# A gated MLP behind linear attention on one core: the whole order of work is written anew

## The chip, the core and the metric

The kernel runs on one core of a Trainium2 chip. The core has a matrix engine (TensorE; PE in the profile, and PEld for its weight loads), VectorE (DVE), ScalarE (ACT), GpSimd (POOL) and SyncE (SP). Each engine takes its own instructions in order, and the engines meet only through semaphores. Here SP issues the loads of q, k and v, the DMA transposes and the stores; GpSimd issues the transfers of the weights. The metric is the device time of one execution in microseconds: lower is better. Three runs of the kernel before gave 149.77, 148.20 and 149.54 us, a median of 149.54.

## What is computed

q, k and v have the shape (4, 8, 768, 64): four batches, eight heads, 768 tokens, 64 columns. Each head has a decay `lam`. First comes linear attention with decay in blocks of 64 tokens, with a running state per head; its output, with the heads side by side, is a matrix of 768 x 512 per batch, and goes through a gated MLP with a spatial product:

```python
for b in range(nb):                      # blocks of 64 tokens
    intra = (qb @ kb.T * Dmask) @ vb
    inter = (qb * lam_pow) @ kv_state
    out[b] = intra + inter
    kv_state = lam_block * kv_state + (kb * rev_pow).T @ vb

h = relu(x @ w_in)                       # 512 -> 1024
u, v = h[:, :512], h[:, 512:]
v_n = (v - mean(v)) / sqrt(var(v) + 1e-6)
v_s = w_spatial @ v_n + b_spatial        # over the 768 tokens
out = (u * v_s) @ w_out                  # 512 -> 512
```

## The kernel before

The tokens are cut into 12 steps of 256 tokens, three to a batch: step n belongs to batch n // 3. A step has all eight heads. Matrix products run in bf16 with sums in fp32. PSUM has eight banks; bank 7 keeps the running state, and the other seven are handed from one piece of work to the next.

The program is a long string, `ORDER`, of 663 short tokens. A loop goes through it and calls for each token one small function, which gives one piece of work to one engine. The token names the function, then the step (or batch) and part, then the PSUM banks, and at the end the engine: T is TensorE, D VectorE, A ScalarE, P GpSimd, S SyncE. So `MK.0.1.0.1.D` is MK for step 0, half 1, from banks 0 and 1, on VectorE. The string alone sets the order on each engine and, for copies, which engine does them; the waits follow from what reads and writes what. The names, in the order in which a step goes through them:

- LQ, LK, LV load a step's q, k, v (512 KB each) into one of three buffers. WI.0 and WI.1 bring the half of W_in for v and that for u; WS.0 and WS.1 the halves of the spatial weights, WO the output weights, BS the bias. GT makes GpSimd wait until a load has landed.
- KM multiplies k by its decay, QC casts q, VC casts v. The work of KM and QC is cut in halves of heads (part 0 and 1; part 2 is both).
- For steps 0 to 4 TK and TQ transpose k and q on TensorE, EK copies the result from PSUM, and EQ copies it and multiplies it by the table that LT writes. For steps 5 to 11 QM multiplies q on VectorE or GpSimd, and DK and DQ transpose by DMA, issued by SP. The transposed k and q have two buffers each, so step n writes where step n - 2 was read.
- SC makes the scores (16 matmuls of 64 x 64), MK multiplies them by the mask. KV adds to the state, SS copies the state out of bank 7. AV.n.0 and AV.n.1 make the output of attention, and FN stands between them; EX copies it into xT.
- PV projects on the half of W_in for v (one 128-token tile each), PU on the half for u (all 256 tokens of two column groups). EV and EU apply relu out of PSUM. BN, RA, RD and VN normalise v.
- WT transposes the spatial weights and EW copies them. When the three steps of a batch are through VN, its eight PW (column group f, token half i) do the spatial product on top of the bias that GP put into the bank; each PW reads the six tiles of its batch that VN wrote. GM multiplies by u.
- PO makes an output tile of 128 tokens from four GM, EO copies it, ST stores it. PH, EH and SH are the same for half a tile, at the end.

The order interleaves three batches at once: while the PW of one batch run, attention for the next has begun, and the PO of the one before are fitted in between.

Of the kernel before, what the change touches and what calls it, by code (L numbers as in the profile page):

```python
# [26 lines left out]
TK.2.1.4.T EK.2.1.4.D EK.2.0.2.A SC.2.0.0.1.T MK.2.0.0.1.D SC.2.1.3.4.T MK.2.1.3.4.D EV.0.0.5.A RA.1.A BN.0.0.D
RA.0.A RD.1.D LV.5.S RD.0.D PU.1.0.6.T PU.1.1.2.T KV.2.0.T SS.2.0.A EU.1.0.6.A AV.2.0.0.1.T FN.2.0.1.D VN.0.0.D
VN.0.1.D PU.0.1.3.T EU.0.1.3.A KM.4.0.P AV.2.1.0.1.T EX.2.0.0.A EX.2.1.1.D GP.0.0.0.4.A EU.1.1.2.A GP.0.0.1.5.A
PU.0.0.6.T EU.0.0.6.D PV.2.0.3.T KM.4.1.P EV.2.0.3.A BN.2.0.D PV.2.1.0.T EV.2.1.0.A BN.2.1.D VN.1.1.D VN.1.0.D  # L30
WT.0.0.1.T WT.1.0.2.T EW.1.0.2.A RA.2.A EW.0.0.1.A RD.2.D VN.2.0.D WT.2.0.6.T EW.2.0.6.A PU.2.0.3.T GP.0.2.0.0.A
PU.2.1.2.T VN.2.1.D WT.1.1.1.T PW.0.0.0.4.T EU.2.0.3.A EU.2.1.2.A EW.1.1.1.A WT.2.1.6.T EW.2.1.6.A GP.0.3.0.3.D
GM.0.0.0.4.D GP.0.1.1.2.A PW.0.2.0.0.T GM.0.2.0.0.D GP.0.1.0.4.A WT.0.1.1.T EW.0.1.1.D PW.0.3.0.3.T TK.3.2.6.T
EK.3.2.6.A TQ.3.2.0.T PW.0.1.0.4.T GM.0.1.0.4.D EQ.3.2.0.D PW.0.1.1.2.T GM.0.1.1.2.D GM.0.3.0.3.D PW.0.0.1.5.T
GM.0.0.1.5.D KV.3.0.T SC.3.0.0.1.T MK.3.0.0.1.D SC.3.1.2.3.T MK.3.1.2.3.D GP.0.2.1.4.A PW.0.2.1.4.T TK.4.2.6.T
QC.4.2.A TQ.4.2.5.T EQ.4.2.5.D GM.0.2.1.4.D GP.0.3.1.0.A PW.0.3.1.0.T AV.3.0.1.2.T FN.3.1.2.D SS.3.0.A KV.3.1.T
KM.5.1.P EK.4.2.6.A SC.4.0.3.4.T GM.0.3.1.0.D KM.5.0.D DK.5.S AV.3.1.1.2.T EX.3.1.2.A EX.3.0.1.A SC.4.1.5.6.T
MK.4.1.5.6.D PO.0.2.0.T EO.0.2.0.A PO.0.4.2.T EO.0.4.2.D QM.5.1.P QM.5.0.D DQ.5.S VC.5.P PO.0.3.1.T PU.3.0.5.T
PV.3.1.6.T PV.3.0.0.T VC.4.A SS.3.1.D KV.4.0.T MK.4.0.3.4.D AV.4.0.2.3.T EV.3.0.0.D BN.3.0.D PO.0.5.4.T
EU.3.0.5.A SS.4.0.A KV.4.1.T EV.3.1.6.A BN.3.1.D LK.6.S KM.6.0.P FN.4.2.3.A AV.4.1.2.3.T EX.4.1.3.D SS.4.1.A  # L40
LV.6.S EX.4.0.2.A RA.3.A RD.3.D PO.0.1.0.T EO.0.1.0.A EO.0.3.1.A KV.5.0.T SC.5.0.5.6.T MK.5.0.5.6.D SC.5.1.2.3.T
# [40 lines left out]
"""


# [475 lines left out]
```

## Time and profile before

| | |
|---|---|
| median of three runs | 149.54 us (148.20 to 149.77) |
| the profiled execution, its own time | 150.31 us |
| its span, first to last instruction | 148.6 us |
| mean granted clock of TensorE | 0.977 |
| TensorE busy | 130.3 us (88% of the span) |
| VectorE, ScalarE, GpSimd busy | 112.8, 83.5, 46.9 us |
| read from and written to HBM | 24.77 and 6.29 MB |
| chain that ended last | TensorE 76%, VectorE 5%, issue 2%, ScalarE 2%, DMA 1% |

The span is what the profiler sees of one execution; the execution's own time has some 1.7 us more around it. Busy time of an engine is time in which at least one of its instructions runs. The chain is followed back from the last instruction, at each step to what released it; "issue" in it is time in which an engine waited for nothing that the profile shows. In the profile's rows an engine's name with a q behind it is its sequencer, which issues DMAs.

### The profile page before, as it was taken

To read this page: it belongs to the slowest core of one execution; us is meant where nothing else is said; L and a number is where in the kernel's file an instruction comes from. 1 tells how busy PE (TensorE), PEld (TensorE's weight loads), DVE (VectorE), ACT (ScalarE), POOL (GpSimd) and SP (SyncE) were. 2 spreads that over 40 slices of the span, in tenths; PEclk is the share of its full clock that TensorE was granted. 3 is DMA by queue.
4 is the path that set the end of the run, shared out by engine and by line. 5 is a ranking of instruction groups with operands and counts; after the bars stand their busy time and mean duration, and the time that the engine had idled before them with its cause. 6 is when DMAs were issued, how large, how long until landed. Compare 5 with 4: busy or idle time off the path is not lost.

```text
span 148.6 us, 4597 instructions
## 1 busy us (share of the span) xinstructions
PE 130.3 (88%) x1933; PEld 84.0 (57%) x1946; DVE 112.8 (76%) x214; ACT 83.5 (56%) x167; POOL 46.9 (32%) x59
## 2 busy tenths in 40 slices
PE   0287368999999999999999999799998999999990
PEld 0166343585776755566766656567663565666530
DVE  4467937798957998799989978967794898696720
ACT  3895710758985474695752658768404446742041
POOL 7593932029600090235050802670822000000000
PEclk9999965999999999999999999999999999999999
DMA  3999999999997015999997999989999487100524
GB/s 88 345 347 346 229 277 220 216 302 292 261 273 210 6 44 113 289 347 242 248 141 225 241 236 349 263 240 259 254 283 137 153 342 294 76 4 0 207 104 183
DMA packets 58376, 32.28 MB, mean 217 GB/s; under 512 B 15859, under 2 KB 55283, under 8 KB 58355
## 3 DMA queue, kind: packets, MB, share of 16 engines
q1 hardware_dynamic: 55968, 29.23, 75.4%
q0 software_dynamic: 2384, 2.75, 10.7%
q8 instruction: 15, 0.25, 0.6%
q14 instruction: 7, 0.05, 0.1%
q10 hardware_dynamic: 2, 0.00, 0.0%
HBM read 24.77 MB, written 6.29 MB: 209 GB/s over the span
## 4 chain that ended last, share of the span: by engine, by line
PE 76%; DVE 5%; issue 2%; ACT 2%; DMA 1%
PE ps L486 21%; PE ps L422 14%; PE ps L460 12%; PE ps L497 12%; PE ps L397 4%; PE ps L367 3%; PE ps L350 3%; PE ps L388 2%; PE ps L319 2%; DVE a_sb L355 2%; PE ps L472 1%; DMA out_dram<-o_sb 1%; DVE vn L451 1%; DVE st L437 1%; DVE xT L178 1%
## 5 line engine op out<-in xcount | busy, mean ns | idle before, releaser
L486 PE MATMUL ps<-wt_sb,vn 128*128 128x384 bf16 x192 | 33.5, 326 | 0.0
L289 POOL TENSOR_TENSOR kc<-k_in,lv 128x512 bf16<-128x512 f32 x18 | 19.3, 1082 | 39.8 <-PE ps L367 12.7
L355 DVE TENSOR_TENSOR a_sb<-ps,m 128x1024 bf16<-128x1024 f32 x24 | 28.7, 1215 | 2.3 <-PE ps L350 2.2
L422 PE MATMUL ps<-win_sb,xT 128*128 128x512 bf16 x92 | 24.6, 401 | 1.4 <-DVE xT L178 1.0
L486 PEld LDWEIGHTS <-vn 128*128 128x128 bf16 x192 | 18.3, 98 | 11.8 <-DVE vn L451 0.6
L460 PE MATMUL ps<-xT,win_sb 128*128 128x256 bf16 x192 | 23.5, 273 | 0.0
L497 PE MATMUL ps<-wout_sb,gT 128*128 128x512 bf16 x83 | 21.9, 380 | 1.2 <-issue 0.9
L492 DVE TENSOR_TENSOR gT<-ps,uT 128x384 bf16<-128x384 f32 x32 | 16.6, 550 | 5.8 <-PE ps L486 4.9
L460 PEld LDWEIGHTS <-win_sb 128*128 128x128 bf16 x192 | 18.1, 98 | 3.9
L437 DVE BATCH_NORM_STATS2 st<-vh 128x6 f32<-128x512 bf16 x24 | 16.5, 688 | 4.6 <-ACT vh L427 4.5
L176 ACT ACTIVATE ps<-bsp 128x384 f32<-128x384 f32 x26 | 12.5, 496 | 9.6 <-DVE gT L492 6.4
L176 ACT ACTIVATE o_sb<-ps 128x512 f32<-128x512 f32 x18 | 10.5, 596 | 12.0 <-PE ps L497 10.5
L427 ACT ACTIVATE vh<-ps 128x512 bf16<-128x512 f32 x19 | 11.3, 595 | 10.3 <-PE ps L422 10.0
L289 POOL TENSOR_TENSOR qc<-q_in,lqn 128x512 bf16<-128x512 f32 x11 | 11.9, 1087 | 15.7 <-DMA q_in<-in_q_dram 8.7
L422 PEld LDWEIGHTS <-xT 128*128 128x128 bf16 x96 | 9.6, 103 | 12.3 <-issue 2.5
L497 PEld LDWEIGHTS <-gT 128*128 128x128 bf16 x92 | 8.3, 98 | 9.9 <-issue 1.0
L176 ACT ACTIVATE xT<-ps 128x512 bf16<-128x512 f32 x15 | 8.5, 595 | 8.1 <-PE ps L397 8.1
L397 PE MATMUL ps<-a_sb,vb 64*64 64x128 bf16 x384 | 11.1, 222 | 1.6 <-issue 1.6
L176 ACT ACTIVATE s_sb<-ps 128x256 bf16<-128x256 f32 x17 | 6.5, 380 | 9.3 <-PE ps L367 9.3
L451 DVE TENSOR_SCALAR vn<-vh,mv,rstd 128x512 bf16<-128x512 bf16 x24 | 11.4, 506 | 0.2
L367 PE MATMUL ps<-vb,kc 64*64 64x64 bf16 x320 | 8.5, 193 | 3.1 <-DVE vb L178 1.8
L427 ACT ACTIVATE uT<-ps 128x512 bf16<-128x512 f32 x17 | 9.8, 590 | 1.7 <-PE ps L460 1.7
(70 smaller groups left out, 159.6 us busy)
## 6 DMA issues: line engine op xcount, KB each, us to landing
k_in<-in_k_dram SPq DMA_DIRECT2D x12, 512.0 KB, 5.7
q_in<-in_q_dram SPq DMA_DIRECT2D x12, 512.0 KB, 6.1
v_in<-in_v_dram SPq DMA_DIRECT2D x12, 512.0 KB, 6.7
out_dram<-o_sb SPq DMA_DIRECT2D x23, 256.0 KB, 3.8
wsp_raw<-in_moe_w_spatial_dram POOLq DMA_DIRECT2D x2, 576.0 KB, 12.4
win_sb<-in_moe_w_in_dram POOLq DMA_DIRECT2D x2, 512.0 KB, 9.5
wout_sb<-in_moe_w_out_dram POOLq DMA_DIRECT2D x1, 512.0 KB, 8.9
bsp<-in_moe_b_spatial_dram SPq DMA_DIRECT2D x1, 384.0 KB, 13.4
```

The costliest lines, as they stand in the source:

```text
L176: nc.scalar.activation(out=o, in_=i, func=AF.Copy)
L289: vec(e).tensor_tensor(out=dst[n % NCA][:, u].rearrange("p u m o d -> p o (u m) d"), in0=src[n % NIN].rearrange("p (o u) m d -> p o u m d" ...
L355: nc.vector.tensor_tensor(out=a_sb[n % NA][:, i].rearrange("p o w j x -> p o w (j x)"), in0=ps[:, b0:b1 + 1:b1 - b0].rearrange("p o (w y) ...
L367: nc.tensor.matmul(out=pkv[row(o), u], lhsT=kc[n % NCA][row(c), u, m, o, :], rhs=vb[n % NCA][row(c), 4 * o + u, m, :], start=new and u == ...
L397: nc.tensor.matmul(out=po[c ^ o][row(w), c, i], lhsT=vb[n % NCA][row(c), 4 * o + u, j, :], rhs=a[row(c), i, o, w, j, :], start=(r == 0 and ...
L422: nc.tensor.matmul(out=bank(b), lhsT=x[:, slot(c, g)], rhs=win_sb[:, g, DH:DFF], start=(g == 0), stop=(g == NCH - 1))
L427: nc.scalar.activation(out=o, in_=i, func=AF.Relu)
L437: nc.vector.bn_stats(out=st6[p2][:, t], in_=vh[p2][:, t])
L460: nc.tensor.matmul(out=pu[:, f2].rearrange("p (c x) -> p c x", c=2), lhsT=win_sb[:, g, f * P:(f + 1) * P], rhs=x[:, slot(0, g):slot(1, g) ...
L486: nc.tensor.matmul(out=bank(b)[:, 0:HW], lhsT=vn[bb % 2][:, s, f * P:(f + 1) * P], rhs=wt_sb[:, s, i * HW:(i + 1) * HW], start=False, stop ...
L492: nc.vector.tensor_tensor(out=gT[bb % 2][:, f, cols], in0=bank(b)[:, 0:HW], in1=uT[bb % 2][:, f, cols], op=ALU.mult)
L497: nc.tensor.matmul(out=bank(b), lhsT=gT[bb % 2][:, f, t * P:(t + 1) * P], rhs=wout_sb[:, f, :], start=(f == 0), stop=(f == NCH - 1))
```

## The change

Only the string `ORDER` differs. Both have the same 663 tokens up to their banks and engines, so the same loads, products, copies and stores. What moves:

- The loads begin with q of steps 0 and 1, then k of both, v of 0, k and q of 2, v of 1. Before it was k and q of 0, k and q of 1, v of 0 and 1.
- The transposes of steps 0 and 1 stand in one run of eight on TensorE, ahead of all scores. Before, scores and transposes of steps 0 and 1 took turns.
- GpSimd casts the four halves of q of steps 0 and 1 first, then one KM, and then issues WI.0, WI.1 and WS.0 one behind the other. Before, casts and multiplications stood between these.
- 86 tokens change engine. VectorE is given in net terms five SS, four VC, three GP, two EK, one KM, one QC, one EU and one EW, and gives away one EX, one EV and one EO. ScalarE has 13 operations fewer, GpSimd two.
- Banks are dealt out anew.
- From step 3 on the interleaving differs too: SC of steps 6 and 7 come earlier among the PW of batch 1, SC of step 11 stand closer behind AV of step 9, and at the end all PW of batch 3 come ahead of all its PH and PO. `one` (a table that nothing reads) moves from the first place to near the end.

The diff, cut to its head, to the parts that the prediction speaks of, and to the end:

```diff
--- before.py
+++ after.py
 ORDER = """
-one.D lam.A LK.0.S msk.P mkc.D LB.0.T LN.0.A posk.P LL.D LX.A KM.0.0.D pos.P idn.P TK.0.0.1.T KM.0.1.P
-TK.0.1.2.T LQ.0.S QC.0.1.D TQ.0.1.3.T LT.0.A QC.0.0.P TQ.0.0.4.T EQ.0.0.4.D LT.1.A EQ.0.1.3.D LK.1.S KM.1.1.P
-TK.1.1.5.T EK.0.0.1.A SC.0.0.3.4.T EK.0.1.2.A LQ.1.S QC.1.0.P EK.1.1.5.A GT.1.1.P WI.0.P KM.1.0.D LV.0.S
-SC.0.1.0.1.T LV.1.S TK.1.0.6.T EK.1.0.6.A TQ.1.0.2.T LQ.2.S LK.2.S QC.1.1.P TQ.1.1.5.T MK.0.0.3.4.D EQ.1.0.2.D
-MK.0.1.0.1.D VC.0.A KV.0.0.T AV.0.0.3.6.T SS.0.0.A FN.0.3.6.A LV.2.S QC.2.1.P BS.S LK.3.S GT.1.2.P WI.1.P
-EQ.1.1.5.D SC.1.1.0.1.T SC.1.0.4.5.T MK.1.0.4.5.D KV.0.1.T SS.0.1.A KM.2.0.P GT.2.1.P WS.0.P LQ.3.S LT.2.A
-AV.0.1.3.6.T LV.3.S LK.4.S VC.1.D KV.1.0.T LQ.4.S SS.1.0.A KV.1.1.T KM.2.1.P LK.5.S MK.1.1.0.1.D AV.1.0.2.4.T
-QC.2.0.A TQ.2.1.5.T EX.0.1.6.D WS.1.P TQ.2.0.0.T EQ.2.0.0.D LQ.5.S VC.2.P FN.1.2.4.A AV.1.1.2.4.T LV.4.S
-EX.1.0.2.D EQ.2.1.5.D EX.1.1.4.A PV.1.0.1.T EX.0.0.3.D SS.1.1.D PV.0.1.6.T EV.0.1.6.A PV.1.1.0.T EV.1.1.0.A
...
-PW.2.1.1.6.T GM.2.1.1.6.D AV.9.0.0.1.T SC.10.0.2.3.T SC.10.1.4.5.T KV.10.1.T FN.9.0.1.D AV.9.1.0.1.T DQ.11.S
-MK.10.0.2.3.D PO.2.2.6.T EO.2.2.6.D ST.1.1.S ST.2.2.S PO.2.5.2.T EX.9.1.1.A EX.9.0.0.A PV.9.0.3.T EV.9.0.3.D
-MK.10.1.4.5.D EO.2.5.2.A PO.1.3.6.T EO.1.3.6.D PV.9.1.1.T EV.9.1.1.A BN.9.1.D SS.10.1.A PO.2.0.0.T EO.2.0.0.A
-ST.2.0.S AV.10.0.3.4.T VC.11.P SC.11.1.5.6.T SC.11.0.1.2.T KV.11.0.T SS.11.0.D FN.10.3.4.A AV.10.1.3.4.T
...
+LQ.0.S msk.P idn.P lam.A LQ.1.S mkc.D pos.P posk.P LB.0.T LN.0.A LK.0.S LK.1.S LL.D LV.0.S QC.0.1.P LX.A
+QC.1.0.P QC.1.1.P QC.0.0.P KM.0.0.D LK.2.S TQ.1.0.1.T LT.1.A LT.0.A KM.1.1.P EQ.1.0.1.D TK.0.0.2.T TQ.0.1.3.T
+KM.0.1.D EK.0.0.2.D KM.1.0.D TK.0.1.4.T EK.0.1.4.A TQ.1.1.5.T TQ.0.0.6.T LT.2.A GT.1.1.P TK.1.0.0.T TK.1.1.1.T
+EQ.0.1.3.D VC.0.D EQ.1.1.5.D WI.0.P EQ.0.0.6.D KV.0.0.T SC.0.1.2.3.T LQ.2.S WI.1.P SC.0.0.4.5.T EK.1.1.1.D
+EK.1.0.0.A MK.0.0.4.5.D SC.1.1.0.1.T LV.1.S SS.0.0.A KV.0.1.T MK.0.1.2.3.D WS.0.P SS.0.1.A SC.1.0.4.5.T KM.2.0.P
+TK.2.0.6.T QC.2.0.A MK.1.1.0.1.D QC.2.1.D VC.1.A AV.0.0.2.3.T FN.0.2.3.A MK.1.0.4.5.D LV.2.S KV.1.0.T LK.3.S
+KM.2.1.P TQ.2.0.0.T AV.1.0.1.4.T FN.1.1.4.A AV.0.1.2.3.T SS.1.0.D AV.1.1.1.4.T EX.1.1.4.A GT.1.2.P WS.1.P
+TQ.2.1.5.T KV.1.1.T EX.1.0.1.D EX.0.1.3.D EX.0.0.2.D PV.1.1.4.T GT.2.1.P TK.2.1.1.T PV.0.0.3.T EV.1.1.4.A
+EK.2.1.1.D PU.1.0.2.T PV.1.0.4.T LV.3.S BS.S EK.2.0.6.A SS.1.1.D EQ.2.0.0.D VC.2.D BN.1.1.D EQ.2.1.5.D KV.2.0.T
...
+LQ.5.S KV.3.0.T VN.2.0.D LK.5.S PU.2.0.5.T VN.2.1.D PW.0.0.0.0.T EU.2.1.6.D GP.0.0.1.6.D EU.0.0.2.A GP.0.2.0.2.A
+PW.0.1.0.3.T QC.4.2.P QC.3.2.D EU.2.0.5.D TQ.3.2.4.T PW.0.0.1.6.T EK.3.2.1.A GM.0.0.0.0.D QM.5.1.P PW.0.2.0.2.T
...
+AV.5.0.0.1.T GP.1.0.0.3.D EV.4.0.6.A VC.6.D FN.5.0.1.D SS.5.0.A PO.0.0.4.T KV.6.0.T EV.4.1.2.A AV.5.1.0.1.T
+PU.4.1.5.T BN.4.0.D EX.5.1.1.A BN.4.1.D PU.4.0.6.T KM.7.1.D VC.7.D RD.3.D EX.5.0.0.A RA.4.A DQ.6.S DK.6.S
+PV.5.1.2.T PV.5.0.1.T RD.4.D VN.4.1.D PU.3.1.0.T EU.4.0.6.A EV.5.1.2.A VN.3.0.D PU.5.1.6.T EU.4.1.5.D VN.4.0.D
+QM.7.0.P EV.5.0.1.A BN.5.1.D EO.0.0.4.A BN.5.0.D SS.6.0.A EU.3.1.0.A DQ.7.S RA.5.A KM.7.0.P VN.3.1.D DK.7.S
+SC.6.0.1.2.T KV.6.1.T RD.5.D SC.6.1.4.5.T LV.8.S VN.5.0.D VN.5.1.D PU.5.0.0.T LK.8.S EU.5.1.6.A MK.6.1.4.5.D
+GP.1.2.1.6.A MK.6.0.1.2.D EU.5.0.0.A KM.8.1.P GP.1.1.1.0.A PW.1.2.1.6.T PW.1.0.0.3.T GP.1.3.1.4.A SS.6.1.D
...
+PW.2.3.0.3.T AV.9.0.0.4.T SC.10.0.5.6.T KV.10.1.T SC.10.1.1.2.T FN.9.0.4.D AV.9.1.0.4.T EX.9.0.0.A GM.2.3.0.3.D
+DQ.11.S VC.11.D EX.9.1.4.A PO.2.1.3.T PO.2.5.0.T SS.10.1.D MK.10.1.1.2.D EO.2.1.3.A PO.1.3.4.T PV.9.0.3.T
+SC.11.1.1.2.T MK.10.0.5.6.D SC.11.0.5.6.T EO.1.3.4.A KV.11.0.T MK.11.1.1.2.D MK.11.0.5.6.D EO.2.5.0.A EV.9.0.3.A
...
+GP.3.3.1.4.A GM.3.2.1.0.D ST.2.4.S PW.3.3.1.4.T PW.3.1.1.2.T PW.3.2.0.3.T GP.3.0.0.6.D GM.3.3.1.4.D ST.2.2.S
+GM.3.1.1.2.D PW.3.1.0.5.T PW.3.0.0.6.T PH.3.5.1.0.T GM.3.3.0.1.D GM.3.1.0.5.D one.D PO.3.4.4.T EO.3.4.4.A
+PO.3.3.2.T GM.3.0.0.6.D GM.3.2.0.3.D ST.3.4.S EH.3.5.1.0.D PH.3.5.0.1.T EH.3.5.0.1.D EO.3.3.2.A PO.3.1.5.T
+EO.3.1.5.D PO.3.0.6.T EO.3.0.6.D SH.3.5.1.S SH.3.5.0.S PO.3.2.3.T ST.3.3.S ST.3.1.S ST.3.0.S EO.3.2.3.A ST.3.2.S
...
```

More of the change, by code (lines that the diff above doesn't have):

```diff
@@ L27 @@
[L27 to L41, printed above, removed]
@@ new lines @@
+SC.4.0.2.3.T KM.5.1.P SS.4.0.A SC.4.1.4.5.T AV.3.1.1.6.T EX.3.0.1.D KV.4.1.T DQ.5.S MK.4.1.4.5.D EX.3.1.6.A
+PO.0.4.0.T PV.3.1.6.T PV.3.0.1.T PO.0.3.4.T EV.3.1.6.A PU.3.0.5.T MK.4.0.2.3.D AV.4.0.2.6.T EV.3.0.1.A
+EO.0.4.0.A VC.5.D BN.3.1.D KM.6.1.D FN.4.2.6.A DK.5.S BN.3.0.D SS.4.1.A EU.3.0.5.D LQ.7.S PO.0.5.3.T KM.6.0.P
+LV.6.S EO.0.3.4.A AV.4.1.2.6.T KV.5.0.T EX.4.1.6.D EO.0.5.3.A LK.7.S QM.6.0.P SC.5.0.0.1.T SC.5.1.4.5.T
+PO.0.1.3.T EX.4.0.2.A PV.4.1.2.T QM.7.1.P MK.5.0.0.1.D EO.0.1.3.A PV.4.0.6.T RA.3.A LV.7.S MK.5.1.4.5.D
@@ new lines @@
+VC.8.A PW.1.1.0.0.T PV.6.0.1.T PV.6.1.6.T GM.1.3.1.4.D EV.6.0.1.A LK.10.S EV.6.1.6.A AV.7.0.2.3.T LK.11.S
+SC.8.1.4.5.T GM.1.1.0.0.D SC.8.0.0.1.T FN.7.2.3.A MK.8.1.4.5.D KV.8.0.T AV.7.1.2.3.T EX.7.1.3.D MK.8.0.0.1.D
+PO.1.5.6.T ST.0.0.S ST.0.3.S EX.7.0.2.A PU.6.1.4.T PO.1.4.5.T LQ.11.S BN.6.0.D AV.8.0.2.3.T VC.9.P PO.1.0.0.T
+FN.8.2.3.D SS.8.0.D KV.9.0.T EO.1.4.5.D AV.8.1.2.3.T KM.10.1.P QM.9.1.D EU.6.1.4.A PV.7.1.1.T LQ.10.S EX.8.0.2.A
+BN.6.1.D KM.10.0.P LV.10.S GP.2.3.1.4.D PU.7.1.5.T PV.7.0.2.T EV.7.1.1.D BN.7.1.D EX.8.1.3.A QM.9.0.P PV.8.0.3.T
@@ new lines @@
+RA.6.A RD.6.D DK.9.S EV.7.0.2.A EO.1.0.0.A PU.8.1.1.T SS.9.0.A PV.8.1.2.T EV.8.0.3.A VN.6.0.D BN.7.0.D
+EV.8.1.2.A EO.1.5.6.A BN.8.0.D RA.7.A KV.9.1.T PU.6.0.0.T BN.8.1.D DQ.9.S VN.6.1.D GP.2.0.1.3.A QM.10.0.P
+EU.6.0.0.A RD.7.D VN.7.1.D VN.7.0.D RA.8.A LV.11.S PO.1.1.2.T RD.8.D PO.1.2.6.T VC.10.P SS.9.1.D VN.8.0.D
+VN.8.1.D QM.11.1.P PU.7.0.0.T QM.10.1.D EU.8.1.1.D EU.7.1.5.A PU.8.0.5.T EU.7.0.0.A EU.8.0.5.A GP.2.1.0.0.D
+ST.0.5.S GP.2.2.1.1.A EO.1.1.2.A PW.2.0.1.3.T PW.2.3.1.4.T DQ.10.S GM.2.0.1.3.D PW.2.2.1.1.T KV.10.0.T DK.10.S
```

62 lines of the change are left out of this document (25 added, 37 removed).

## The prediction

> **What bounds the kernel now.** I read the utilisation rows first, then busy time by stretch, then the chain of work in order of time. The page's rows:
>
> ```profile
> PE 130.3 (88%) x1933; PEld 84.0 (57%) x1946; DVE 112.8 (76%) x214; ACT 83.5 (56%) x167; POOL 46.9 (32%) x59
> ...
> q8 instruction: 15, 0.25, 0.6%
> ...
> qT<-qc SPq DMA_TRANSPOSE x7, 4.6
> ```
>
> Busy time by stretch (start:end, its length, then busy us and instructions of PE, PEld, DVE, ACT, POOL, granted clock, DMA share, GB/s):
>
> ```profile
> 0.00:23.00 23.00, 11.33 (x259) 8.77 (x260) 14.11 (x25) 13.62 (x29) 14.72 (x27) 0.93 1.03 270
> 23.00:30.00 7.00, 6.50 (x59) 3.22 (x59) 5.28 (x11) 3.21 (x5) 1.03 (x1) 0.75 1.15 218
> 30.00:140.00 110.00, 107.63 (x1596) 69.80 (x1606) 91.84 (x177) 64.24 (x130) 31.16 (x31) 1.00 0.85 209
> ```
>
> From 30 to 140 us TensorE is busy 107.6 of 110 us: it is the bound there, and all but 2.4 us is work that the change leaves as it is. Before 23 us it is busy 11.3 of 23, and from 23 to 30 its clock is at 0.75. So there are three places where a new order can gain or lose: the first 23 us, the 2.4 us of holes in the dense part, and new holes.
>
> The chain of work in order of time (start, length, what), its dense part:
>
> ```profile
> 94.15 0.81 issue
> ...
> 99.13 2.62 PE ps L460 x24
> 101.75 4.88 PE ps L486 x30
> ...
> 112.82 0.55 issue
> ...
> 116.14 0.86 PE ps L422 x4
> 117.00 0.86 PE ps L497 x4
> 117.86 0.24 PE ps L388 x8
> 118.10 0.22 PE ps L397 x16
> 118.32 0.45 PE ps L350 x32
> 118.77 0.18 PE ps L367 x12
> ```
>
> The rows run end to end: no operand is late. They also give the price of each piece of TensorE work at full clock: PV and PO 0.86, PU 2.62/3 = 0.87, PW 4.88 x 6/30 = 0.98, AV 0.24 + 0.22 = 0.46, SC 0.45/2 = 0.23, KV 0.18 x 16/12 = 0.24. The two large holes are "issue", where TensorE waits for nothing that another engine does.
>
> I read these two as instruction fetch. TensorE has 1946 weight loads and as many matmuls, and 15 packets carried instructions: 259 instructions, some 129 pairs, in a packet. Counted along the order, the hole at 94.15 stands behind about 1383 pairs (inside AV.8.1), that at 112.82 behind about 1634 (inside PO.2.2) and an early one, shown below at 19.77, behind about 223 (inside AV.1.0). Their distances are 1160 and 251 pairs, 9 and 2 packets: all three stand where a packet ends. By the prices above, the packet's worth of pairs ahead of them holds 5.0, 5.7 and 1.9 us of work, less than any other packet of this order (5.9 and up). Runs of 64x64 matmuls use up instructions fast, and the next packet comes too late.
>
> **The change, part by part.** No instruction is added or removed; all 663 steps stand in both orders. Work changes engine and place.
>
> *TensorE in the dense part.* Both orders have 17 runs of KV, SC and AV behind the first PW, and the same sums. What shifts is which work falls into which packet. In the new order the packets that hold pairs 1248 to 1376 and 1504 to 1632 carry 7.0 and 7.5 us instead of 5.0 and 5.7, and the shortest behind the head is 5.6 (pairs 608 to 736), then 6.2. A packet of 5.9 showed no hole before. I take both holes as gone: 0.81 + 0.55 = **-1.36 us**. The ends: nothing gained if the packet of 5.6 and those of 6.2 stop in their stead, all of it if none does; I take the end to which the row of 5.9 without a hole is nearer.
>
> The Trainium skill, "Runtime: NRT & Kernel Launch", section "Instruction fetch mechanics", says that the sequencer fetches the next block while it runs this one, so that crossing a block boundary is mostly hidden. By that rule the holes have another cause and stay, and the term is 0 instead of -1.36. The trace speaks for blocks of the size that the page gives, but against "hidden": three ends of packets have a hole.
>
> *The head.* Rows of the timeline (start, length, engine, line, what; in brackets the idle time before it):
>
> ```profile
> 1.94 1.37 SPq L191 DMA_DIRECT2D k_in<-in_k_dram  x1
> ...
> 10.16 0.92 POOL L247 DMA_DIRECT2D win_sb<-in_moe_w_in_dram  x1
> ...
> 16.14 1.15 DVE L178 CAST vb<-v_in 128x1024 bf16<-128x1024 f32 x1
> 16.68 0.63 POOL L243 COPY seen<-v_in 1x1 f32<-1x1 f32 x1
> ...
> 19.77 0.32 PE L397 MATMUL ps<-a_sb,vb 64*64 64x128 bf16 x3 [0.80 <-issue]
> ...
> 21.93 0.69 DVE L178 CAST xT<-ps 128x512 bf16<-128x512 f32 x1 [0.35 <-PE ps L397]
> ...
> 22.67 0.61 PE L422 MATMUL ps<-win_sb,xT 128*128 128x512 bf16 x1 [0.83 <-DVE xT L178]
> ```
>
> The issue groups, for the load at 1.94 and for the first half of W_in (last column: us from issue to landing):
>
> ```profile
> k_in<-in_k_dram SPq DMA_DIRECT2D x1, 512.0 KB, 5.8
> ```
>
> ```profile
> win_sb<-in_moe_w_in_dram POOLq DMA_DIRECT2D x1, 512.0 KB, 9.6
> ```
>
> And VectorE's groups from 6 to 23 us (count, busy us, mean ns, idle before):
>
> ```profile
> L355 DVE TENSOR_TENSOR a_sb<-ps,m 128x1024 bf16<-128x1024 f32 x4 | 4.9, 1219 | 0.9 <-PE ps L350 0.7
> L333 DVE TENSOR_TENSOR qT<-ps,lq 128x512 bf16<-128x512 bf16 x6 | 2.4, 420 | 3.7 <-ACT seen L176 2.1 <-ACT lq L223 1.3 <-PE ps L319 0.2
> L178 DVE CAST xT<-ps 128x512 bf16<-128x512 f32 x3 | 2.0, 681 | 0.3 <-PE ps L397 0.3
> L289 DVE TENSOR_TENSOR kc<-k_in,lv 128x512 bf16<-128x512 f32 x2 | 1.4, 688 | 1.3 <-ACT lv L219 1.3
> ```
>
> Before, the first V projection starts at 22.67, right behind the second half of xT at 21.93, and W_in's half has been there since 10.16 + 9.6 = 19.8. With q0 and q1 first, k0 is the third load; the third load before was issued at 1.94 and landed 5.8 later, at 7.7. From there VectorE's queue is the path. Up to the end of EX.1.0 it holds three KM (0.69), four EQ and two EK (0.42, EK by the row of EQ), VC.0 (1.15), four MK (1.22), half a QC (the kernel shows none undisturbed; as KM, 0.69), one SS (0.42 as EQ) and EX (0.68): 2.07 + 2.52 + 1.15 + 4.88 + 0.69 + 0.42 + 0.68 = 12.4. Two waits stand inside: MK.0.0 for its scores, 0.7 by the idle column of MK, and EX.1.0 for three AV behind MK.1.0, 3 x 0.46 less the SS beside it, and less where the AV overlap: 0.6. So EX.1.0 ends at 7.7 + 12.4 + 1.3 = 21.4 and PV.1.1 starts there. The 0.80 us fetch hole falls beside this path: its pair 223 is now in AV.1.1, and the packet ahead of it has 2.2 us of work that is spread over the waits for VectorE.
>
> The other engines keep up. GpSimd issues W_in behind five operations, the last of which waits for k1, so at about 10.6 instead of 10.16, and the half lands at 20.2. The second half, issued right behind it, comes no sooner than before: the DMA share is 1.15 from 23 to 30 us, full, and earlier issue only lengthens the queue. v1 is now the eighth load instead of the sixth, 3 us later at some 1.5 us a load (the issues on SP, 1.4 us each); VC.1 is due before MK.1.0 ends and hides that by some 2 us.
>
> At PV.1.1 the new order has done about 0.2 us more work (one half of TK.2), so the head gives 22.67 - 21.4 + 0.2 = **-1.5 us**. The ends: 0 if W_in's half and VectorE's queue are each a microsecond later, -2.3 if VectorE's operations overlap as closely as the best pairs do. I take the middle, as the queue is a sum of rows. It need not all arrive: behind it SC.2.1 waits for EQ.2.1, which now stands behind BN.1.1 on VectorE; I put that wait, some 0.9, beside the waits of 28 to 30 us before and count it in the range.
>
> *Waits that are added.* (1) QC.3.2 goes from GpSimd to VectorE, directly between VN.2.1, which the first PW needs, and TQ.3.2, two PW later. EU as EX, GP between EQ and EX, and a whole QC as VC (0.68 + 0.55 + 1.15) are 2.4 us against 2 x 0.98 = 2.0: **+0.4**, between 0 and 0.9. Behind QC.3.2 on VectorE stand EU.2.0 and the first GM, with a bank's time to spare. (2) The DMA transpose of step 11's q may be issued when AV.9.1 has read the buffer that it overwrites. Then came six PO and PV and one AV before SC.11 (5.6 us); now it is four (3.5). With 4.6 us to landing: 4.6 - 3.5 - 0.2 (the last matmuls of AV no longer read it) = **+0.9**, between 0 and 2. SP's queue is free there: the one store ahead of it waits for nothing.
>
> *VectorE's load.* It takes over five SS, four VC, three GP, and net one KM, QC and two EK, and gives away some evictions: 2.1 + 4.6 + 1.7 + 0.7 + 1.1 + 0.8 - 0.8 = 10 us more at most. Some 7 of that fall into the dense part, where VectorE has 110 - 91.8 = 18 us idle. I cost it at nothing; the cover is that idle time.
>
> *The end* keeps its shape: 2.6 us of PH and PO lie between the last PW and the PO that needs its GM, against 1.1 us of GM; the last store follows an eviction on ACT as before. No term.
>
> **Sum**: -1.5 - 1.36 + 0.4 + 0.9 = -1.6 us. It is made against the profiled execution (span 148.6, its own time 150.31), which lies 0.8 above the median 149.54; that difference carries over, so 149.54 - 1.6 = **147.9 us**. A difference of about 1%, 1.5 us, is what this kernel's runs can tell from none.
>
> **Rivals.** *The holes move* (chance 0.23): fetch stops TensorE elsewhere, or the holes aren't fetch. For it: packets of 5.6 and 6.2 us, and one long run of six KV, SC and AV behind AV.3.0. Against it: packets of 5.9 to 6.3 ran through before. Sum -0.2: 149.3.
>
> *VectorE becomes the bound* (0.30), the case on the slower side. Its place is the stretch from PO.0.1 to PW.1.0.1: VC.6 and VC.7 now stand in VectorE's queue ahead of the six VN that PW.1 waits for, and behind these MK.6, SS.6.1 and GM free the banks of SC.7 and AV.6. By full durations without overlap that queue is 9.6 us from AV.5.0 to VN.5.1, where TensorE has 9.0, and VC.6 holds up its start. It decides once VectorE runs its operations at over 0.9 of their durations; then each later product starts late, 1.4 us at PW.1, as much again at SC.7 to PW.1.0.1, and half of that at PW.2 and PW.3, where VectorE carries 27 and 30 us a batch by these durations against TensorE's 27 and 29. Some 4 us in all: 151.9. Against it: VectorE's 18 us of idle time.
>
> *The clock returns earlier* (0.10).
>
> ```profile
> 23.50 3.85 PE ps L422 x10
> ```
>
> Here ten matmuls of a V projection take 0.385 each, against 0.216 in the dense rows; by the clocks of the stretches the half clock lasts 0.07 x 23 / 0.5 = 3.2 us ahead of 23 us and 0.25 x 7 / 0.5 = 3.5 us behind it, so to about 26.5. If TensorE, busier from 19 us on, gets its clock back 3.4 us sooner, it does 1.5 us more work by then: 146.4. The Trainium skill, "TensorE: Matmul & The Clock Gate", Part 1, speaks of a free-running window of about 3.4 us; by that it depends on the phase of a run. The trace's low stretch of 6.7 us is two such windows and agrees.
>
> **Chances.** Forecast 0.37, at 147 to 148.7; about a third of that lies within 1%. Faster by over 1%: 0.25 + 0.10 + 0.05 of the holes' case = 0.40; within 1%: 0.12 + 0.18 of the holes' case = 0.30; slower: 0.30. The range takes in the clock's case and VectorE's: 145.8 to 152.2. The likeliest case's own range is 147 to 148.7.
>
> **What the new profile would show.** The first V projection near 21.4 us, behind EX.1.0 on VectorE; no "issue" piece over 0.3 us inside AV.8 or behind AV.9.1; SC.11 waiting about 0.9 for the transpose of q; TQ.3.2 waiting for VectorE's QC; VectorE near 121 us busy. Wrong would make it: an idle TensorE ahead of PW.1 with VN.5.1 as releaser, W_in's half landing behind 22 us, or "issue" pieces in the run behind PO.0.2.

## The result and the profile after

The new kernel takes 148.22 us (median of 20 runs, 147.12 to 150.19) where before takes 149.25 (20 runs, 148.2 to 150.62). The ratio is 0.9932, interval 0.9904 to 0.996: faster by 0.7%, about 1 us, and by no more than 1.0%. The forecast was 147.9, range 145.8 to 152.2. The profiled execution of the new kernel took 148.72 us, 1.59 less than the one of before (150.31). So the traces compared below differ by 0.6 us more than the medians do.

The utilisation row of the new kernel's page:

```profile
PE 130.0 (88%) x1929; PEld 84.2 (57%) x1946; DVE 117.4 (80%) x229; ACT 75.7 (51%) x154; POOL 46.0 (31%) x57
```

Busy time by stretch, columns as in the prediction:

```profile
0.00:23.00 23.00, 12.80 (x266) 9.26 (x268) 13.89 (x26) 12.23 (x26) 13.63 (x26) 0.91 1.03 265
23.00:30.00 7.00, 6.95 (x83) 4.29 (x83) 5.50 (x12) 4.26 (x7) 1.70 (x2) 0.80 1.15 217
30.00:140.00 110.00, 107.08 (x1570) 69.17 (x1583) 96.16 (x189) 57.99 (x120) 30.72 (x30) 1.00 0.80 210
```

TensorE has 1.5 us more behind it at 23 us (12.80 against 11.33) and 0.45 more in the next 7 us. In the dense part it is busy half a microsecond less than before. VectorE is busy 4.6 us more in all, not 10, and at 117.4 us stays under the 121 that the prediction named.

A finer reading: take the start of a product (its first weight load) and subtract the work of all products ahead of it, at the prices of the prediction. Four pieces have no price there; rows of these traces give 0.45 for eight transposes of k or q, 0.42 for a WT, 0.50 for a PH and 0.22 for an AV that has no state to add. What is left is the time that TensorE has lost by then. At points with about the same work done, worked out from the two traces:

```
work ahead     5.8    12.5    35.2    53.0    70.0    76.5    85.7    91.6    98.4   120.2 us
before       16.94   19.66   20.04   20.80   21.03   22.28   22.54   23.31   23.31   23.40
after        15.35   17.66   17.90   18.65   19.12   19.38   21.16   21.21   21.86   21.74
difference   -1.59   -2.00   -2.14   -2.15   -1.91   -2.90   -1.38   -2.10   -1.45   -1.66
```

The head leads by 1.6 at the first PV and by 2.0 to 2.15 from there to 53, and hands on some 1.9 at 70. (Differences of 0.2 are runs of 64x64 matmuls that fall on either side of a point.) The single steps in this bookkeeping: before loses 1.0 in AV.8.1 and 0.7 in PO.2.2 (its chain calls 0.81 and 0.55 of that "issue"), and the new kernel 1.5 between 76 and 86 and some 0.45 behind 91. -1.9 - 1.7 + 1.5 + 0.45 is -1.65, and the last products start 1.66 apart. The chain of work of the new kernel shows the body's places:

```profile
88.01 0.31 PE ps L366 x12
88.38 0.06 PE ps L387 x4
88.44 0.05 PE ps L396 x2
88.49 0.22 PE ps L396 x14
...
100.91 0.68 DVE uT L428
101.59 0.02 issue
101.61 0.50 ACT ps L175
102.12 0.04 issue
102.16 1.14 PE ps L485 x6
...
110.33 4.00 DMA qT<-qc
114.33 0.14 issue
114.46 0.63 PE ps L349 x30
```

The first four rows are KV.9.0 and AV.8.1, without the hole that before has there. At 102.16 PW.2.2.1 starts late: its bank was prefilled at 101.61, behind EU.8.1.1 on VectorE at 100.91. At 114.46 SC.11 starts when the transpose of q has landed. The line numbers are one less than before, since the new order fills one line less.

### The profile page after: what moved, and what is told of

Read it like the earlier page. It is cut to its first block, busy times and chain, and to the rows that moved or that the text cites. A ratio compares the mean times of both kernels' runs of the same rounds, so it can differ in the third digit from the quotient of the medians.

```text
span 147.0 us, 4585 instructions
## 1 busy us (share of the span) xinstructions
PE 130.0 (88%) x1929; PEld 84.2 (57%) x1946; DVE 117.4 (80%) x229; ACT 75.7 (51%) x154; POOL 46.0 (31%) x57
## 4 chain that ended last, share of the span: by engine, by line
PE 80%; DMA 7%; SPq 5%; DVE 3%; issue 2%; ACT 1%; DVEq 0%
PE ps L485 22%; PE ps L459 15%; PE ps L421 14%; PE ps L496 12%; SPq L190 5%; DMA q_in<-in_q_dram 4%; PE ps L396 4%; PE ps L349 4%; PE ps L366 3%; PE ps L387 3%; DMA qT<-qc 3%; DVE a_sb L354 2%; PE ps L318 2%; PE ps L471 2%; PE ps L505 1%
## 5 line engine op out<-in xcount | busy, mean ns | idle before, releaser
L485 PE MATMUL ps<-wt_sb,vn 128*128 128x384 bf16 x192 | 33.0, 326 | 1.3 <-ACT ps L175 1.3
L421 PE MATMUL ps<-win_sb,xT 128*128 128x512 bf16 x90 | 23.9, 399 | 0.7 <-issue 0.6
L459 PE MATMUL ps<-xT,win_sb 128*128 128x256 bf16 x192 | 24.3, 275 | 0.0
L426 ACT ACTIVATE vh<-ps 128x512 bf16<-128x512 f32 x20 | 12.0, 599 | 14.6 <-PE ps L421 14.6
L175 ACT ACTIVATE o_sb<-ps 128x512 f32<-128x512 f32 x19 | 11.1, 593 | 14.4 <-PE ps L496 14.4
L175 ACT ACTIVATE xT<-ps 128x512 bf16<-128x512 f32 x16 | 9.2, 596 | 11.6 <-PE ps L396 11.2
L175 ACT ACTIVATE ps<-bsp 128x384 f32<-128x384 f32 x23 | 11.0, 491 | 5.3 <-DVE uT L428 2.7
L450 DVE TENSOR_SCALAR vn<-vh,mv,rstd 128x512 bf16<-128x512 bf16 x24 | 10.9, 476 | 0.3
L396 PE MATMUL ps<-a_sb,vb 64*64 64x128 bf16 x384 | 10.2, 221 | 0.3 <-DVE a_sb L354 0.3
L349 PE MATMUL ps<-qT,kT 64*64 64x128 bf16 x384 | 9.2, 219 | 1.2 <-DVE a_sb L354 0.8
```

What stands on the lines that cost most here:

```text
L175: nc.scalar.activation(out=o, in_=i, func=AF.Copy)
L349: nc.tensor.matmul(out=pa[o][row(c), w, j], lhsT=kT[n % NTR][row(o), u, j, c * Q64:(c + 1) * Q64], rhs=qv(n, o, u, c), start=(w == 0 and j ...
L396: nc.tensor.matmul(out=po[c ^ o][row(w), c, i], lhsT=vb[n % NCA][row(c), 4 * o + u, j, :], rhs=a[row(c), i, o, w, j, :], start=(r == 0 and ...
L421: nc.tensor.matmul(out=bank(b), lhsT=x[:, slot(c, g)], rhs=win_sb[:, g, DH:DFF], start=(g == 0), stop=(g == NCH - 1))
L426: nc.scalar.activation(out=o, in_=i, func=AF.Relu)
L459: nc.tensor.matmul(out=pu[:, f2].rearrange("p (c x) -> p c x", c=2), lhsT=win_sb[:, g, f * P:(f + 1) * P], rhs=x[:, slot(0, g):slot(1, g) ...
```

## Experiments

Each was timed beside runs of before on the same chip (149.37 to 149.44 us there); ratios are to those. Only the kernel before itself, run again, has a single time.

### The head alone (h1_newhead), and the body alone (h2_oldhead)

```diff
 TK.4.2.4.T GM.0.2.1.2.D PO.0.2.0.T
-AV.3.0.1.6.T EQ.4.2.3.D KM.5.0.P GM.0.1.1.5.D KV.4.0.T EK.4.2.4.A
+one.D GM.0.1.1.5.D EQ.4.2.3.D AV.3.0.1.2.T FN.3.1.2.D KM.5.1.P
...
```

The rest of this list is what before has left, in its order. The second kernel is the reverse, cut behind MK.3.1.

> The new order up to the first PO of batch 0 (some 50 us), from there the order of before. The two traces put 2.0 us of the gain into the head (TensorE has the same work done 2.0 us earlier at 50 us) and the body at -1.35 for the two fetch holes, +0.5 for SC.11's wait and +1.4 for a new wait ahead of PW.2.2.1, together +0.5. Theory: the head alone gives 2.0 us, so 147.2 us where before has 149.25, and the holes in AV.8.1 and PO.2.2 are back, 0.8 and 0.5 us. Rival (the gain of the head is given back later, by transfers or VectorE that come later): 148.5 to 149.3 us, with TensorE idle between 50 and 90 us.

Measured: 148.39 us, ratio 0.9956 (0.9923 to 0.9988), so 1.0 us faster by the medians and not 2.0; that is nearer to the rival's case. In its profile the head's lead is there and more (PO.0.2.0 starts at 48.33 us, in the new kernel at 49.28, whose half clock ended 3.9 us later), and 2.4 us of new losses follow, 1.1 behind the seam and 1.3 around SC.6, at 75 to 79 us. So it is no clean measure of the head. One thing in it I had not expected. AV.8.1, which has the hole in before, runs through; weight loads of TensorE:

```profile
93.08 0.14 PEld L387 LDWEIGHTS <-s_sb 64*64 64x64 bf16 x8 [0.21 <-issue]
93.16 0.28 PEld L396 LDWEIGHTS <-vb 64*64 64x64 bf16 x16
...
110.08 1.41 PEld L496 LDWEIGHTS <-gT 128*128 128x128 bf16 x8
```

The 16 loads of AV.8.1 follow each other, though a packet ends among them as in before, and so do the eight of PO.2.2 and PO.2.5. Why is shown with the packets below. Behind the seam both kernels have the same products in the same order, so the starts of one can be subtracted from those of the other without any price. Its lead over before is 0.7 us from 79 us up to AV.8.1, 1.7 behind AV.8.1 and 2.4 behind PO.2.2 and at the end: in this profile 1.7 us of the lead are the two holes, which the expectation had put back.

> The order of before up to the MK of step 3 (some 47 us), from there the new order. Theory: the body of the new order is 0.5 us worse than that of before, so 149.7 us (149.3 to 150.2): no holes in AV.8.1 and PO.2.2, but the wait of 1.2 to 1.4 us ahead of PW.2.2.1 and that of SC.11, 0.8, are there. Rival (the body carries the gain, the head's lead is noise of the one profile): 148.2 us.

Measured: 154.1 us, ratio 1.0335 (1.0275 to 1.0394). Far off both cases, and the cause is the seam: TensorE waits for the prefill of banks there, and loses 2.9 us by the bookkeeping.

```profile
50.30 1.14 PE L485 MATMUL ps<-wt_sb,vn 128*128 128x384 bf16 x6 [1.64 <-ACT ps L175]
...
52.66 1.14 PE L485 MATMUL ps<-wt_sb,vn 128*128 128x384 bf16 x6 [0.86 <-ACT ps L175]
```

For the size of the body this kernel says nothing. Only single waits can be read: the one ahead of PW.2.2.1 is there (0.81), SC.11's transpose too (0.34).

### The two holes: instruction fetch or something else (b_pad112s, before2, a_pad64)

```diff
-mkc.D LB.0.T LN.0.A
+mkc.D LB.0.T FL.112.8.5.1.T LN.0.A
...
-            nc.tensor.matmul(out=bank(b)[:, 0:w], lhsT=ones[:, 0:P], rhs=ones[:, 0:w],
-                             start=(new == 1 and i == 0), stop=True, skip_group_check=True)
+            nc.tensor.matmul(out=bank(b)[row(i % 2), 0:w], lhsT=ones[row(i % 2), 0:Q64], rhs=ones[row(i % 2), 0:w],
+                             start=True, stop=True, skip_group_check=True)
```

> Before, with 112 tiny 64x64 matmuls behind LB, in the time in which TensorE waits for the first transpose; their product is overwritten. They shift every end of a packet of instructions 112 pairs earlier in the order. In the traces of before and of the new kernel the next packet's first instruction follows 1.3 to 1.4 us behind the landing of its packet wherever there is a hole, and the landing lies 0 to 5.0 us behind the start of the packet ahead. If the holes in AV.8.1 and PO.2.2 are instruction fetch they vanish from both places, and with the ends of packets that the shift gives (near 82, 89, 95, 107, 117, 123 us) at most one short hole is left: 149.3 - 1.36 = 147.9 us (147.3 to 148.3). If they are anything else, they stay in AV.8.1 and PO.2.2: 149.3 us, or more if the added matmuls delay the first transpose.

Measured: 148.46 us, ratio 0.9952 (0.9924 to 0.998), 0.9 us faster than before, from matmuls that compute nothing. Both places run through. The row at AV.8.1, and behind it the early hole, which has moved with its packet:

```profile
93.13 0.28 PEld L397 LDWEIGHTS <-vb 64*64 64x64 bf16 x16
```

```profile
19.30 0.42 PE L388 MATMUL ps<-qT,s_sb 64*64 64x128 bf16 x5
21.08 0.32 PE L388 MATMUL ps<-qT,s_sb 64*64 64x128 bf16 x3 [1.36 <-issue]
21.09 0.73 PE L397 MATMUL ps<-a_sb,vb 64*64 64x128 bf16 x16
22.64 0.61 PE L422 MATMUL ps<-win_sb,xT 128*128 128x512 bf16 x1 [0.82 <-DVE xT L178]
```

The early hole is 1.36 us here, and yet the first V projection starts at 22.64, as before (22.67): it waits for xT anyway. So that hole costs nothing, as the prediction had it. The products stand in the same order as in before, so starts can be compared without prices again: this trace leads the first profile of before by 0.8 us ahead of AV.8.1 (0.3 of it came with a half clock that ended 0.55 us sooner), by 1.74 behind AV.8.1 and by 2.46 behind PO.2.2, loses 0.5 at PV.9.1 and SC.11, and ends 1.95 ahead. The two holes are 0.95 and 0.72 of that, 1.7 together. The 0.9 of the medians is the change as a whole, with those new losses in it; what the two holes cost in an execution near the median no run shows by itself.

> The kernel before, profiled once more. Its execution of the first profile took 150.31 us against a median of 149.3, and the two holes there were 1.36 us of it. If the fetch of a packet depends on what is in the DMA queues at that moment, the landing 5.0 us behind the start of the packet is the long end of a spread, and in an execution nearer to the median the holes in AV.8.1 and PO.2.2 are shorter or missing: 0 to 0.8 us together. If it depends on the order alone, both are there again with 0.8 and 0.55 us.

```profile
93.82 0.16 PEld L397 LDWEIGHTS <-vb 64*64 64x64 bf16 x5
94.99 0.20 PEld L397 LDWEIGHTS <-vb 64*64 64x64 bf16 x11 [1.00 <-issue]
...
112.85 0.55 PEld L497 LDWEIGHTS <-gT 128*128 128x128 bf16 x4 [0.49 <-issue]
```

Before once more, 150.17 us: both holes are there again, 1.00 in the weight loads at AV.8.1 and 0.49 at PO.2.2. Compared with b_pad112s they cost 1.03 and 0.17, against 0.95 and 0.72 in the first profile: the same places, other lengths. Both executions lie some 0.8 above the median. The traces hold each packet of instructions with its times. Beside them the first weight load that the packet brings, counted 128 pairs to a packet (at PO.2.2 the pause ends two loads sooner, at 113.37, 1.41 behind the landing):

```
kernel, end of packet       start of packet   landed    next load   behind landing   hole
before, AV.1.0                        14.01    18.45        19.78             1.33   yes
before, AV.8.1                        88.52    93.55        94.96             1.41   yes
before, PO.2.2                       106.99   111.95       113.60             1.65   yes
before2, AV.8.1                       88.47    93.71        94.99             1.29   yes
new, AV.1.1                           13.19    18.13        19.52             1.40   0.45
new head, old body, AV.8.1            87.81    91.72        93.23             1.50   none
new, PV.7.0                           83.25    87.11        90.61             3.50   none
new, PO.2.5                          103.78   105.96       111.50             5.54   none
```

In the 13 profiles 183 ends of packets can be looked at so. Never does the next load come less than 1.29 us behind the landing. In the ten ends at which the weight loads pause for 0.4 to 1.75 us and the landing is near, it comes 1.29 to 1.65 behind it; six pauses of 0.52 at other ends stand 3.6 us or more behind a landing and are the usual ones between long matmuls. Whether a hole stands at an end is a race between the work in the packet and the fetch: the landing lies between -0.8 and 5.2 us behind the start of the packet ahead, and differs from execution to execution (5.04 in before, 3.91 in the kernel with the new head, for the same packet with the same 5.0 us of work ahead of its end). So the holes are fetch, and they are not a fixed price.

> The new kernel with 64 tiny matmuls behind LB, which shift the ends of packets 64 pairs earlier: a packet of 4.4 us of work (82.3 to 86.7 us, up to AV.8.0) arises, the only one behind 30 us under 5 us. With a landing 2.7 to 4.6 us behind the start of the packet and 1.4 us more, TensorE stands there for 0 to 1.7 us, 0.9 by the landing nearest in time (3.9). Theory: 0.9 us slower than the new kernel, 149.1 us (148.2 to 149.9), the hole at the end of that packet in the profile. If holes aren't instruction fetch: none there, 148.2 us.

```diff
-LB.0.T LN.0.A
+LB.0.T FL.64.8.5.1.T LN.0.A
```

(with the same FL, and its `one` at the head of the list). Measured: 147.86 us, ratio 0.9896 (0.9849 to 0.9943), no slower than the new kernel. The short packet was made, and no hole came of it. Its successor landed at 81.98, ahead of the packet's start at 82.78. The rule "landing plus 1.3 or more" holds, but how late a landing is can't be read from the nearest packet in time. In this profile one step that the prediction had priced shows as well:

```profile
41.64 0.62 PE L319 MATMUL ps<-ident,qc 128*128 128x128 bf16 x8 [0.54 <-DVE qc L178]
```

TQ.3.2 waits 0.54 for VectorE's QC.3.2. In the new kernel's own profile it doesn't:

```profile
39.43 1.95 PE ps L485 x12
41.38 0.45 PE ps L318 x8
41.83 3.90 PE ps L485 x24
```

### W_in's halves together (a_wi_apart, c2_pu, c3_wt)

```diff
-EQ.1.1.5.D WI.0.P EQ.0.0.6.D KV.0.0.T SC.0.1.2.3.T LQ.2.S WI.1.P SC.0.0.4.5.T
+EQ.1.1.5.D WI.0.P EQ.0.0.6.D KV.0.0.T SC.0.1.2.3.T LQ.2.S SC.0.0.4.5.T
...
-GT.1.2.P WS.1.P
+GT.1.2.P WI.1.P WS.1.P
```

> The new kernel with the second half of W_in issued where before had it, behind v1's landing, some 4 us later, and all else as new. If the half together with the first is a part of the gain, the first PU waits for it: landing at 24.9 + 2 to 4 us, so 1.5 to 4 us slower, 149.7 to 152 us. By the prediction (the DMA queues are full anyway, earlier issue only lengthens the queue) it lands at 24 to 25 us as in before, and the time stays within 0.5 of 148.2 us.

Measured: 154.33 us, ratio 1.0306 (1.0239 to 1.0372). The first PU, TensorE:

```profile
28.61 1.68 PE L459 MATMUL ps<-xT,win_sb 128*128 128x256 bf16 x7 [3.67 <-DMA win_sb<-in_moe_w_in_dram]
```

It waits 3.67 us for the half, issued at 16.2 and landed 12.4 later, and starts 3.6 later than in the new kernel, whose row is this (weight loads):

```profile
24.98 1.02 PEld L459 LDWEIGHTS <-win_sb 128*128 128x128 bf16 x6 [0.56 <-DMA win_sb<-in_moe_w_in_dram]
```

The prediction's "earlier issue only lengthens the queue" was half right. Early issue (12.3, and 12.6 us to landing) brings the half at 24.9, no sooner than in before (issued at 14.6, 9.4 us to landing: 24.0). But with the loads in their new order a late issue costs the whole delay, and more: behind the wait TensorE runs at half clock a second time, and the delay grows from 3.6 us at the first PU to 5.7 at 34.5 us. The stretch, columns as in the prediction:

```profile
27.20:34.00 6.80, 5.39 (x63) 3.21 (x64) 1.60 (x5) 1.74 (x3) 2.85 (x3) 0.50 1.13 292
```

The kernel loses some 6 us in all. The new kernel's own row shows what ends its head: the first PU starts when W_in's second half lands. The same with QM.10.1 moved (next section), a profile in which the half clock ended at 22.0 us instead of 25.8:

```profile
24.93 1.05 PE L459 MATMUL ps<-xT,win_sb 128*128 128x256 bf16 x8 [1.18 <-DMA win_sb<-in_moe_w_in_dram]
```

TensorE was ahead and waited for the rest, 1.18 us. This is where an earlier clock goes.

```diff
-PU.1.0.2.T PV.1.0.4.T
+PV.1.0.4.T PU.1.0.2.T
```

> As c1_qm_sc11, and PU.1.0 behind PV.1.0 instead of ahead of it. With QM.10.1 on GpSimd the first PU started at 24.93 us, just when the second half of W_in landed, with 1.4 us of idle TensorE ahead of it, although the half clock had ended 3.8 us sooner than in the profile of the new kernel. If W_in's second half is what ends the head, PV.1.0 fills that time: 0.9 us less than c1_qm_sc11 when the clock is back early, 0 when it is not: 0.3 to 0.9 less in the median. If TensorE's own work at half clock or VectorE's queue ends the head, no change.

Measured: 146.95 us against 146.90 without this exchange (c1_qm_sc11, below): no gain. PV.1.0 fills the wait, and the next transfer takes the gain back. WT.0.1, TensorE:

```profile
32.52 0.84 PE L472 MATMUL ps<-ident,wsp_raw 128*128 128x128 bf16 x12 [0.84 <-DMA wsp_raw<-in_moe_w_spatial_dram]
```

```diff
-EX.2.0.3.A WT.1.1.1.T EX.2.1.4.D EW.0.0.2.A EW.0.1.6.A PV.2.0.0.T PV.2.1.3.T VN.1.1.D EW.1.1.1.D
+EW.0.0.2.A EX.2.0.3.A EX.2.1.4.D PU.0.0.2.T PV.2.0.0.T PV.2.1.3.T WT.0.1.6.T WT.1.1.1.T VN.1.1.D
...
```

> As c2_pu, and WT.0.1 and WT.1.1, which need the second half of W_spatial, behind PV.2.1; PU.0.0 fills their place and TK.3.2 goes behind PU.2.0. In c2_pu TensorE stood 1.0 us ahead of WT.0.1. If that half's landing (near 32.4 us) is what took back the gain of c2_pu, 146.2 us (146.0 to 146.5); if the head's lead is given back behind it as well, 146.9 us as before.

Measured: 151.42 us, ratio 1.0126 (1.0072 to 1.018): 4.5 us slower than without it. Both expectations fall. WT came later, so did the evictions of the weights, and VectorE's VN of step 2 met GpSimd's work. GpSimd, then VectorE, then TensorE in that stretch:

```profile
41.25 1.03 POOL L289 TENSOR_TENSOR kc<-k_in,lv 128x512 bf16<-128x512 f32 x1
42.24 1.03 POOL L180 CAST qc<-q_in 128x1024 bf16<-128x1024 f32 x1
```

```profile
40.45 2.97 DVE L451 TENSOR_SCALAR vn<-vh,mv,rstd 128x512 bf16<-128x512 bf16 x2
43.34 0.68 DVE L429 TENSOR_SCALAR uT<-ps 128x512 bf16<-128x512 f32 x1
43.48 1.31 PE L486 MATMUL ps<-wt_sb,vn 128*128 128x384 bf16 x7 [1.16 <-DVE vn L451]
```

Two VN took 2.97 us, one of them 2.25, where VN takes 0.38 to 0.42 when GpSimd does nothing. It ends 0.15 us behind the second of GpSimd's operations, and PW.0 waits for it. How the rest of the 4.5 us splits I did not settle.

### The wait ahead of PW.2.2.1 (a_qm_pool, a_eu_first)

```diff
-QM.10.1.D
+QM.10.1.P
```

> The new kernel with QM.10.1 back on GpSimd. Theory: the 1.26 us ahead of PW.2.2.1 is VectorE's queue: QM.10.1 (1.53 us there, beside GpSimd's QM.11.1) stands ahead of EU.8.1.1, which frees the bank that GP.2.2.1 and PW.2.2.1 need; without it the wait goes and the kernel takes 148.2 - 1.3 = 146.9 us. Rival: VectorE is late by its whole load (96 of 110 us busy between 30 and 140 us), and the wait moves to the next product: 148.0 to 148.4 us.

Measured: 147.09 us, ratio 0.9858 (0.9805 to 0.991), 1.1 us faster than the new kernel. The wait is gone; TensorE goes through 17 matmuls of PW.2 from 98.33 on:

```profile
98.33 2.93 PE L485 MATMUL ps<-wt_sb,vn 128*128 128x384 bf16 x17
```

```diff
-QM.10.1.D EU.8.1.1.D
+EU.8.1.1.D QM.10.1.D
```

> The new kernel with one exchange in VectorE's queue: EU.8.1.1 ahead of QM.10.1, which stays on VectorE. If the 1.26 us ahead of PW.2.2.1 comes from the order of that queue (QM.10.1, 1.53 us, stood between a finished PU.8.1 and the operation that frees its bank), the wait goes as with QM.10.1 on GpSimd: 147.1 us. If it comes from what VectorE has to do in all, QM.10.1 delays the next operation instead, and the time stays near 148.2 us.

Measured: 147.38 us, ratio 0.9864 (0.9818 to 0.9911). So it is the order of VectorE's queue, not its whole load: with the same operations on the same engine and two of them exchanged, nearly all of the wait goes. In the new kernel's timeline, VectorE, GpSimd, ScalarE and TensorE stand so:

```profile
98.29 1.09 POOL L288 TENSOR_TENSOR kc<-k_in,lv 128x512 bf16<-128x512 f32 x1
...
99.34 1.09 POOL L288 TENSOR_TENSOR qc<-q_in,lqn 128x512 bf16<-128x512 f32 x1
99.45 1.53 DVE L288 TENSOR_TENSOR qc<-q_in,lqn 128x512 bf16<-128x512 f32 x1
100.90 0.68 DVE L428 TENSOR_SCALAR uT<-ps 128x512 bf16<-128x512 f32 x1
...
101.61 0.49 ACT L175 ACTIVATE ps<-bsp 128x384 f32<-128x384 f32 x1 [2.14 <-DVE uT L428]
...
102.16 0.32 PE L485 MATMUL ps<-wt_sb,vn 128*128 128x384 bf16 x1 [1.26 <-ACT ps L175]
```

QM.10.1 on VectorE started 0.1 us behind GpSimd's QM.11.1 and took 1.53 us instead of the 0.68 to 0.72 of such operations; EU.8.1.1, whose product had long been done, stood behind it.

### SC.11's wait (c1_qm_sc11)

```diff
-PV.9.0.3.T SC.11.1.1.2.T
+PV.9.0.3.T PV.9.1.0.T SC.11.1.1.2.T
...
-AV.10.0.0.4.T ST.2.5.S PO.2.0.3.T
+AV.10.0.3.4.T PO.2.0.0.T
...
```

> The new kernel with QM.10.1 on GpSimd, and PV.9.1 ahead of SC.11 (banks 0 and 3 exchanged from there on). The wait of SC.11 for the transpose of q, 0.77 us in the trace, 0.3 of it in before too, is covered by the 0.86 us of PV.9.1. Theory: 0.5 us less than with QM.10.1 alone (147.1), so 146.6 us. Rival (MK of step 11 on VectorE then is late for AV.11.0, and the time is given back there): 147.1 us.

Measured: 146.9 us, ratio 0.986 (0.9811 to 0.9909); 0.2 less than with QM.10.1 alone, which can't be told from nothing. The wait itself is gone, TensorE (the first row has PV.9.0 and PV.9.1):

```profile
111.57 1.89 PE L422 MATMUL ps<-win_sb,xT 128*128 128x512 bf16 x8
113.39 0.64 PE L350 MATMUL ps<-qT,kT 64*64 64x128 bf16 x32
```

This kernel and c2_pu have the lowest medians of all, 1.4 and 1.5% faster than before by their ratios, where the new kernel is 0.7% faster; neither can be told from the one with QM.10.1 alone.

## Why the prediction was right, point by point

- **Direction and size.** -1.6 was forecast against the profiled execution, and the profiled executions differ by 1.59; the medians differ by 1.0. That the sum came out is luck in good part. By the bookkeeping its terms are -1.9 for the head instead of -1.5, -1.7 for the holes instead of -1.36, 0 for QC.3.2 instead of +0.4, +0.45 for SC.11 instead of +0.9, and +1.5 at PW.2.2.1, where nothing had been priced.
- **The head, -1.5 forecast.** The first PV starts at 21.30 (forecast 21.4); the lead is 1.6 there, 2.0 to 2.15 behind it and 1.9 where the dense part's own steps begin. Some 0.4 of it may be the half clock, which ended at 25.8 us in this profile and at 26.55 in that of before (an estimate: half of the difference). The time of the first PV was right and the mechanism wrong. VectorE's queue was to be the path up to EX.1.0. The trace, VectorE:

```profile
11.32 0.68 DVE L177 CAST vb<-v_in 128x1024 bf16<-128x1024 f32 x1
...
16.64 0.42 DVE L177 CAST qc<-q_in 128x512 bf16<-128x512 f32 x1
16.97 1.22 DVE L354 TENSOR_TENSOR a_sb<-ps,m 128x1024 bf16<-128x1024 f32 x1
18.11 0.41 DVE L177 CAST s_sb<-ps 128x256 bf16<-128x256 f32 x1
20.34 1.89 DVE L177 CAST xT<-ps 128x512 bf16<-128x512 f32 x3 [1.82 <-PE ps L396]
```

  VectorE was done with its last MK by 18.2 and then waited 1.82 us for TensorE, which did three AV, part of them at half clock and with the fetch hole among them; 0.6 had been allowed for it. What made up for it is VectorE's queue: VC.0 took 0.68 and not 1.15, half a QC 0.42 and not 0.69. The 1.15 had been read from a VC that began while GpSimd worked. Behind the first PV neither engine is the limit but W_in's second half, which the prediction had left out of the path.
- **The two holes, -1.36.** Both are gone, and they are fetch, as was said: the shift alone takes them away, and each ends 1.29 to 1.65 us behind the landing of a packet. But the work in the packet alone does not decide, as the prediction reckoned: 5.0 us of work had a hole in before and none with the new head, and a_pad64's short packet had none. The size was read too small: 1.7 in the first profile of before, 1.2 in the second. The rule of the Trainium skill, "Runtime: NRT & Kernel Launch", section "Instruction fetch mechanics", that the crossing of a block is mostly hidden, agrees with 173 of the 183 ends of packets and not with the ten where the fetch lands late.
- **QC.3.2 on VectorE, +0.4.** 0 in the new kernel's profile, 0.54 in a_pad64. Within the bounds of 0 to 0.9.
- **SC.11, +0.9.** SC.11 starts 0.77 behind the work of PV.9.0; before loses 0.3 ahead of AV.10.0 and SC.11 too, so some +0.45: oversized, since the transpose took 4.0 us and not 4.6. The place of the wait and what it is for were right.
- **VectorE becomes the bound (0.30, slower).** It didn't between PO.0.1 and PW.1, where the rival had its place and from where 4 us were to come. But it did for one bank, at PW.2.2.1, for 1.26 us of idle TensorE, 1.4 by the start of the product behind it compared with a_qm_pool. There the step "I cost it at nothing; the cover is that idle time" failed: idle time elsewhere is no cover for an operation that stands between a finished product and the release of its bank.
- **The clock returns earlier (0.10).** The length of the half clock differs between profiles: it ends at 25.8 us in the new kernel and at 22.0 with QM.10.1 on GpSimd. The first PU starts at 24.98 and 24.93. So the 1.5 us that this case was given don't come through to the PU.

## What to carry to other kernels

Ask of a moved operation what stands behind it in its engine's queue, and first of all which operation there frees a bank: an operation of 0.7 us in the wrong place, slowed to 1.53 there, cost 1.26 us of TensorE. A duration taken from a row is only good for the company in which it ran. And where an engine is busy to 98%, holes that nothing explains are worth a count of instructions: a few that do nothing, placed where the engine waits anyway, tell whether it is the fetch.
